# The fifth chunk of keys: 128 rows with zeros in place of 64 rows, in 32 small products of an attention and feed-forward kernel

## The chip, the cores and the metric

The kernel runs on one core of one Trainium2 chip. The metric is the device time of one execution in microseconds (us): the median of several runs of the same program. TensorE is called PE in the profile (PEld for its weight loads), VectorE DVE, ScalarE ACT, GpSimd POOL and SyncE SP.

## What is computed

Eight batches of eight heads, 576 tokens and a head size of 64 go through a linear attention; its output, 4608 tokens of width 512, goes through a feed-forward layer of width 2048 with a gated activation.

```python
q_s = exp(q - max over d);        q_s /= sum over d + 1e-9
k_s = exp(k - max over tokens);   k_s /= sum over tokens + 1e-9
kv  = einsum('bhsd,bhse->bhde', k_s, v)          # sum over 576 tokens
attn = einsum('bhsd,bhde->bhse', q_s, kv)
h = x @ w_in;  g = h * clip(h + 3, 0, 6) / 6;  out = g @ w_out
```

The change touches the line of `kv`: a sum over 576 tokens, which is 4 chunks of 128 tokens and one of 64.

## The kernel before

**The parts.** The 4608 tokens are worked in two ways. The first 1536 go in three blocks of 512 (`j` = 0, 1, 2; `TB` = 512): for each of 16 slices `f` of the hidden width, `gemm1` makes `ph` (12 matmuls of 128x512), an activation and a split into two parts give `gp`, and `gemm2` adds to the output banks `po` (12 matmuls). The other 3072 tokens go in three big blocks of 1024 (`s` = 0, 1, 2) through `phase1` and `phase2`, products with fewer multiplications whose banks are called `x`, `y` and `z`. In block 0 the weights are also brought in and decoded, slice by slice (`load_w`, `decode`): `raw` is what the DMA brings, `m` and `v` are steps of the decoding on ACT and DVE, `w` is the pair of parts that the matmuls use; for odd slices from 3 on the second part of `w` is made on POOL instead of DVE.

**The attention beside it.** The attention of the next block is cut into four units, one for each pair of heads `hp`, and woven into the matmuls of the block that runs. A unit of `attention(j, hp)` loads keys (`kt`), values (`vt`) and queries (`qt`), takes the softmax of the keys (`k_softmax`), turns them on the PE (`pe` for the first four chunks, `pe2` for the fifth), and copies them on ACT into `ke`. Then it turns the queries (`tp`, copied to `qT`), makes `pkv` with `kv_of`, normalises it on DVE (`rk`, then `kv`), makes `px` and splits it into `x`. In `sb_attention`, for the big blocks, the keys come from memory already turned, in chunks of 128 with the last 64 tokens padded by a value whose exponential is zero; `ke` is written whole, by one load, one subtraction and one exponential. `vt` is padded with zeros in memory in both.

**The products in question.** `kv_of` is called 32 times: 4 times for block 0, 4 each for blocks 1 and 2, and 20 times from `sb_attention` (for the first two big blocks two batches in a row for each pair of heads, so 8 double calls; for the last big block one, so 4 single calls). A call has 5 chunks and 2 heads, 10 matmuls; each of these float32 matmuls appears in the trace as two passes, so 20 passes a call and 640 in all. The two heads write to the lower and the upper 64 rows of `pkv`. In chunks 0 to 3 a matmul takes 128 rows, and in chunk 4 only the 64 rows that hold tokens.

**What sets the order.** The order of the instructions on each engine is chosen ahead of time by a scheduler with a model of its own; from block 1 on the matmuls keep the order in which the program writes them (`in_order`), while the other engines, and the PE in block 0, may be reordered. Tiles with `bufs=2` such as `ke` are used in turn: a unit writes its `ke` once the product two units ago has read it. All engines execute their own lists strictly in order.

Of the kernel before, what the change touches and what calls it, by code (L numbers as in the profile page):

```python
# [18 lines left out]
P = 128  # L19
TB = 512  # L20
QD = 32
NC4 = TB // P
# [10 lines left out]
def attention_moe(  # L33
# [15 lines left out]
    nc = tc.nc  # L49

    B, NP, _, S = kT.shape
    D = q.shape[5]
# [7 lines left out]
    NCH = S // P + 1  # L60
    TAIL = S % P
# [14 lines left out]
    def bank_a(name):  # L76
        return ps_a.tile([P, TB], F32, name=name, tag="pa")
# [3 lines left out]
    def ordered(ins):  # L81
        if in_order:
            tc.keep_in_program_order(ins)

    def mm(out, lhsT, rhs, start, stop, goes_on=False):
        ordered(
            nc.tensor.matmul(  # L87
                out, lhsT, rhs, start=start, stop=stop, skip_group_check=goes_on
            )
        )  # L90

    def flip(out, in_):
        ordered(nc.tensor.transpose(out, in_, ident))
# [94 lines left out]
    def kv_of(j, hp, ke, vt):  # L188
        pkv = bank_a("pkv")
        for c in range(NCH):  # L190
            r = slice(0, P if c < NC4 else TAIL)
            for h in range(2):
                hs = slice(h * D, (h + 1) * D)
                mm(pkv[hs, 0 : D + 1], ke[r, c, hs], vt[r, c, h, :], c == 0, c == NCH - 1)
        rk = att.tile([P, 1], F32, name="rk", bufs=2)
        nc.vector.tensor_scalar_add(rk, pkv[:, D : D + 1], EPS)
        nc.vector.reciprocal(rk, rk)
        kv = att.tile([P, P], F32, name="kv", bufs=10)
        nc.vector.scalar_tensor_tensor(
            kv.rearrange("p (h d) -> p h d", h=2),  # L200
            pkv[:, 0:D].rearrange("p (o d) -> p o d", o=1).broadcast_to([P, 2, D]),
            rk,
            mask.rearrange("p (h d) -> p h d", h=2),
            op0=ALU.mult,
            op1=ALU.mult,
        )
        kvs[j, hp] = kv
# [29 lines left out]
    def k_softmax(j, km, ke, kt):  # L237
        nc.vector.tensor_reduce(km, kt, axis=AX.X, op=ALU.max, negate=True)
        nc.scalar.activation(kt, kt, AF.Exp, bias=km)
        yield  # L240
        a = bank_a if j else bank
        pe, pe2 = a("pe"), a("pe2")
        for c in range(NC4):
            flip(pe[:, c * P : (c + 1) * P], kt[:, c * P : (c + 1) * P])
        flip(pe2[0:TAIL, 0:P], kt[:, TB:S])
        nc.scalar.copy(ke[:, 0:NC4].rearrange("p c n -> p (c n)"), pe)
        nc.scalar.copy(ke[0:TAIL, NC4], pe2[0:TAIL, 0:P])

    def attention(j, hp):

        if not j:
            kt, qt, qT, vt, ke = first[hp]
        else:
            kt, ke, vt = load_k(j, hp)
            qt = att.tile([P, TB], F32, name="qt", bufs=1)
            nc.sync.dma_start(qt, q[j, hp])
            qt = qt.rearrange("p (c h d) -> p c h d", c=NC4, h=2)
        km = att.tile([P, 1], F32, name="km", bufs=2)
        ks = k_softmax(j, km, ke, kt)
        next(ks)  # L260
        q_softmax(qt, j > 0, nc.vector if j else nc.gpsimd)
        yield
        next(ks, None)
        tp = (bank_a if j else bank)("tp")
        for c in range(NC4):
            flip(tp[:, c * P : (c + 1) * P], qt[:, c].rearrange("p h d -> p (h d)"))
        if j:
            qT = att.tile([P, TB], F32, name="qT")
        nc.scalar.copy(qT, tp)
        yield  # L270
        kv_of(j, hp, ke, vt)
        yield
        px = (bank_a if j else bank)("px")
        e = SHIFT * j
        for b, lo, hi in ((j - 1, 0, e), (j, e, TB)):
            if lo < hi:
                mm(px[:, lo:hi], kvs[b, hp], qT[:, lo:hi], True, True)
        x_hi, x_lo = x_block(j)
        split(x_hi[:, hp, :], x_lo[:, hp, :], px)
# [51 lines left out]
    def sb_attention(s, hp):  # L331
# [24 lines left out]
        for b, (ke, vt, kb) in new.items():  # L356
            kv_of(b, hp, ke, vt)
# [502 lines left out]
```

## Time and profile before

| | |
|---|---|
| median of 3 runs | 872.07 us (871.47 to 872.77) |
| the profiled execution's own time | 867.29 us |
| its span, first to last instruction | 865.5 us |
| busy: PE, PEld | 819.9, 657.5 us (95%, 76%) |
| busy: DVE, ACT, POOL | 674.1, 459.1, 68.2 us (78%, 53%, 8%) |
| mean granted PE clock | 0.988 |

The profiled execution is 4.8 us shorter than the median of the runs, and its span 1.8 us shorter than its own time. Busy shares are averages over parts with different limits. In a timeline, each row is a start, a length, an engine, a line of the kernel, an operation and its output and inputs; rows of like instructions are merged with their count, so that a merged row's length ends with the end of its last instruction. Matmuls are pipelined: the start of the next one says more about the rate than the length of one. "128\*64" behind a matmul is the number of rows and columns of the PE array that it uses.

### The profile page before, as it was taken

The numbers are of one execution on the slowest core, as the hardware profiler recorded it, in microseconds if no ns is written. First come the engines' busy times: TensorE is split into PE (matmuls) and PEld (weight loads), VectorE is DVE, ScalarE is ACT, GpSimd is POOL, SyncE is SP. The second block draws the span as 40 slices with busy tenths as digits, with TensorE's granted clock in tenths as the row PEclk, the third lists the DMA queues.
The fourth block names the chain that finished last, engine by engine and source line by source line (L and its number), as shares of the span: only waits on it lengthen the run. The fifth ranks groups of instructions, "written<-read, shape, count | busy, mean of one in ns | idle before, by whom it ended". The sixth has DMA issues, their size and how long they took to land.

```text
span 865.5 us, 11820 instructions
## 1 busy us (share of the span) xinstructions
PE 819.9 (95%) x4064; PEld 657.5 (76%) x4064; DVE 674.1 (78%) x1064; ACT 459.1 (53%) x789; POOL 68.2 (8%) x142
## 2 busy tenths in 40 slices
PE   5789998899999998999998999999999999999997
PEld 4568776677887876888786787777788788887886
DVE  7998997885957889579988986588597846648763
ACT  7887665554434445355555553554555634444543
POOL 5111211000100110101102000011000000000000
PEclk9889999999999999999999999999999999999999
DMA  9997654675639661488775566765556775555572
GB/s 368 413 409 265 219 181 161 210 258 201 226 139 316 223 228 58 135 286 266 267 261 176 190 219 226 240 223 172 164 179 195 228 237 194 195 193 191 193 234 87
DMA packets 73531, 190.99 MB, mean 221 GB/s; under 512 B 7168, under 2 KB 19456, under 8 KB 71424
## 3 DMA queue, kind: packets, MB, share of 16 engines
q1 hardware_dynamic: 72896, 189.20, 63.8%
q10 hardware_dynamic: 576, 1.05, 0.3%
q8 instruction: 32, 0.52, 0.3%
q14 instruction: 27, 0.22, 0.1%
HBM read 146.18 MB, written 44.04 MB: 220 GB/s over the span
## 4 chain that ended last, share of the span: by engine, by line
PE 60%; DVE 16%; DMA 5%; issue 4%; ACT 3%; POOL 1%; ACTq 0%; DVEq 0%; SPq 0%; POOLq 0%
PE x L87 25%; PE y L87 10%; PE z L87 9%; PE po L87 7%; PE ph L87 6%; DVE g L498 2%; DVE gp L121 1%; DMA kt<-in_kT_dram 1%; PE px L87 1%; DMA wf<-gp 1%; PE pkv L87 1%; ACT qt L221 1%; DMA out_dram<-v 1%; DMA v<-whole 1%; POOL swap L303 1%
## 5 line engine op out<-in xcount | busy, mean ns | idle before, releaser
L120 ACT CAST gf<-g 128x512 fp32r<-128x512 f32 x168 | 104.2, 624 | 96.4 <-DVE gf L121 48.6
L87 PE MATMUL po<-w,gp 128*128 128x512 f32 x576 | 145.1, 400 | 5.3 <-DVE gp L121 4.3
L87 PE MATMUL ph<-x,w 128*128 128x512 f32 x576 | 144.9, 399 | 2.7 <-POOL w L121 1.3
L121 DVE TENSOR_TENSOR gf<-g,gf 128x512 fp32r<-128x512 f32 x168 | 113.3, 689 | 31.7 <-ACT gf L120 31.0
L87 PEld LDWEIGHTS ph<-x,w 128*128 128x128 f32 x576 | 109.8, 192 | 28.6 <-POOL w L121 1.7
L87 PEld LDWEIGHTS po<-w,gp 128*128 128x128 f32 x576 | 107.3, 190 | 30.2 <-DVE gp L121 5.4
L87 PE MATMUL x<-right,gp 128*128 128x512 f32 x384 | 95.0, 392 | 2.8 <-DVE g L538 2.8
L87 PE MATMUL x<-gf,gp 128*128 128x512 f32 x384 | 89.0, 389 | 0.0
L87 PEld LDWEIGHTS x<-right,gp 128*128 128x128 f32 x384 | 71.6, 188 | 19.1 <-DVE g L538 3.6
L87 PEld LDWEIGHTS x<-gf,gp 128*128 128x128 f32 x384 | 72.1, 188 | 15.0
L497 ACT ACTIVATE g<-ph,three 128x512 f32<-128x512 f32 x48 | 33.0, 691 | 67.7 <-PE ph L87 67.7
L497 ACT ACTIVATE v<-g,three 128x1024 f32<-128x1024 f32 x24 | 27.7, 1154 | 39.6 <-DVE g L542 39.6
L87 PE MATMUL x<-right,left 128*128 128x512 f32 x192 | 47.8, 392 | 0.8 <-DVE g L538 0.8
L87 PE MATMUL y<-right,gp 128*128 128x512 f32 x192 | 48.2, 395 | 0.0
L120 ACT CAST gp<-g 128x512 fp32r<-128x512 f32 x48 | 29.8, 622 | 33.4 <-DVE g L498 30.7
L87 PE MATMUL z<-gf,gp 128*128 128x512 f32 x192 | 45.8, 392 | 0.9 <-DVE gf L121 0.8
L87 PE MATMUL x<-gf,left 128*128 128x512 f32 x192 | 45.9, 392 | 0.8 <-DVE gf L121 0.7
L498 DVE SCALAR_TENSOR_TENSOR g<-g,ph 128x512 f32<-128x512 f32 x48 | 32.4, 677 | 15.4 <-ACT g L497 15.3
L87 PEld LDWEIGHTS z<-gf,gp 128*128 128x128 f32 x192 | 35.7, 188 | 10.0 <-DVE gf L121 2.6
L87 PEld LDWEIGHTS x<-gf,left 128*128 128x128 f32 x192 | 35.7, 188 | 9.7 <-DVE gf L121 2.5
L87 PEld LDWEIGHTS x<-right,left 128*128 128x128 f32 x192 | 35.7, 188 | 8.6 <-DVE g L538 1.3
L87 PEld LDWEIGHTS y<-right,gp 128*128 128x128 f32 x192 | 35.6, 188 | 8.0 <-issue 0.5
(135 smaller groups left out, 1323.3 us busy)
## 6 DMA issues: line engine op xcount, KB each, us to landing
gp<-wf SPq DMA_DIRECT2D x112, 512.0 KB, 3.4
left<-wf SPq DMA_DIRECT2D x56, 512.0 KB, 3.5
raw<-in_w_dram SPq DMA_DIRECT2D x16, 1024.0 KB, 14.2
wf<-gp SPq DMA_DIRECT2D x64, 256.0 KB, 2.6
wf<-w SPq DMA_DIRECT2D x48, 256.0 KB, 4.1
vt<-in_v_dram SPq DMA_DIRECT2D x28, 325.0 KB, 5.5
kt<-in_kT_dram SPq DMA_DIRECT2D x28, 288.0 KB, 3.5
ke<-in_k_dram SPq DMA_DIRECT2D x20, 320.0 KB, 4.9
```

The costliest lines, as they stand in the source:

```text
L87: nc.tensor.matmul(out, lhsT, rhs, start=start, stop=stop, skip_group_check=goes_on)
L120: nc.scalar.copy(hi, src)
L121: engine.tensor_sub(lo, src, hi.bitcast(F32))
L221: nc.scalar.activation(qs[:, i], qs[:, i], AF.Exp, bias=qm[:, i : i + 1], accum_out=qr[:, i : i + 1],)
L303: nc.gpsimd.tensor_copy(swap[r : r + QD], stat[o : o + QD])
L497: nc.scalar.activation(r, h, AF.Relu, bias=three, scale=1.0)
L498: nc.vector.scalar_tensor_tensor(g, r, 6.0, h, op0=ALU.min, op1=ALU.mult)
```

## The change

`kv_of` takes all 128 rows in the fifth chunk as well. In `k_softmax` the upper 64 rows of that chunk of `ke` are set to zero on POOL, since no copy writes them there; the upper rows of `vt` are zero already. In `sb_attention` nothing has to be added.

```diff
     def kv_of(j, hp, ke, vt):
         pkv = bank_a("pkv")
         for c in range(NCH):
-            r = slice(0, P if c < NC4 else TAIL)
             for h in range(2):
                 hs = slice(h * D, (h + 1) * D)
-                mm(pkv[hs, 0 : D + 1], ke[r, c, hs], vt[r, c, h, :], c == 0, c == NCH - 1)
+                mm(pkv[hs, 0 : D + 1], ke[:, c, hs], vt[:, c, h, :], c == 0, c == NCH - 1)
...
         nc.scalar.copy(ke[:, 0:NC4].rearrange("p c n -> p (c n)"), pe)
         nc.scalar.copy(ke[0:TAIL, NC4], pe2[0:TAIL, 0:P])
+        nc.gpsimd.memset(ke[TAIL:P, NC4], 0.0)
```

The number of matmuls stays; 12 memsets are added (blocks 0, 1 and 2, four units each). Because the scheduler lays out the program anew, the lists of the engines also move: on the PE only within block 0, on DVE, ACT and SP mostly there and by a few places in block 1.

POOL's list from block 0's decoding to its end, before (`w_3_422` is the decoded slice 3, and so on; this is the second part of `w` for the odd slices):

```order
L121 TENSOR_TENSOR w_3_422<-v_418,w_3_422 128x2x512
L121 TENSOR_TENSOR w_5_534<-v_530,w_5_534 128x2x512
L121 TENSOR_TENSOR w_7_686<-v_681,w_7_686 128x2x512
L121 TENSOR_TENSOR w_9_821<-v_816,w_9_821 128x2x512
L121 TENSOR_TENSOR w_11_972<-v_967,w_11_972 128x2x512
L121 TENSOR_TENSOR w_13_1074<-v_1069,w_13_1074 128x2x512
L121 TENSOR_TENSOR w_15_1165<-v_1160,w_15_1165 128x2x512
```

The same place after, where the memsets belong to the units of blocks 1 and 2:

```order
L247 MEMSET ke_544 64x128
L121 TENSOR_TENSOR w_3_426<-v_422,w_3_426 128x2x512
L121 TENSOR_TENSOR w_5_539<-v_535,w_5_539 128x2x512
L121 TENSOR_TENSOR w_7_692<-v_687,w_7_692 128x2x512
L247 MEMSET ke_697 64x128
L121 TENSOR_TENSOR w_9_828<-v_823,w_9_828 128x2x512
L121 TENSOR_TENSOR w_11_980<-v_975,w_11_980 128x2x512
L247 MEMSET ke_849 64x128
L121 TENSOR_TENSOR w_13_1082<-v_1077,w_13_1082 128x2x512
L247 MEMSET ke_1289 64x128
L121 TENSOR_TENSOR w_15_1173<-v_1168,w_15_1173 128x2x512
```

Three memsets now stand between the seven splits and one right ahead of them; five others stand further up, at the start of the program, and three behind the last split.

DVE's list near the start of block 0, where the last of the four units there is normalised (`rk_293`, then `kv_296`), before:

```order
L196 TENSOR_SCALAR rk_293<-pkv_282 128x1
L121 TENSOR_TENSOR w_1_334<-v_330,w_1_334 128x2x512
L121 TENSOR_TENSOR x0_311<-px_314,x0_311 128x512
L141 SCALAR_TENSOR_TENSOR v_362<-raw_2_118,m_358 128x1024
L197 RECIPROCAL rk_293<-rk_293 128x1
L121 TENSOR_TENSOR x0_311<-px_318,x0_311 128x512
L145 ISA v_362<-raw_2_118,v_362 128x2048
L199 SCALAR_TENSOR_TENSOR kv_296<-pkv_282,rk_293,mask_80 128x128
```

The same steps on DVE after (`rk_297`, then `kv_300`):

```order
L195 TENSOR_SCALAR rk_297<-pkv_286 128x1
L121 TENSOR_TENSOR x0_315<-px_318,x0_315 128x512
L196 RECIPROCAL rk_297<-rk_297 128x1
L134 TENSOR_SCALAR m_362<-m_362 128x1024
L198 SCALAR_TENSOR_TENSOR kv_300<-pkv_286,rk_297,mask_80 128x128
```

Three big steps of the decoding (`w_1`, and `v` of slice 2 twice) have moved from between `rk` and `kv` to behind them.

The PE's list where block 0 ends and block 1 begins, before (`x_311` is the input of block 0, `x_564` that of block 1, `w_1122` and `w_1165` are slices 14 and 15, `w_306` is slice 0):

```order
L87 MATMUL po<-w_1074,gp 128x512 x4
L87 MATMUL ph<-x_311,w_1165 128x512 x10
L87 MATMUL ph<-x_564,w_306 128x512 x9
L87 MATMUL px<-qT,kv 128x448
L87 MATMUL ph<-x_564,w_306 128x512 x3
L87 MATMUL po<-w_1122,gp 128x512 x12
L87 MATMUL po<-w_1165,gp 128x512 x12
```

And after (`x_315` and `x_569` are the inputs, `w_1130` and `w_1173` slices 14 and 15, `w_310` slice 0):

```order
L87 MATMUL px<-qT,kv 128x448
L87 MATMUL ph<-x_315,w_1173 128x512 x2
L87 MATMUL ph<-x_569,w_310 128x512 x12
L87 MATMUL po<-w_1130,gp 128x512 x9
L87 MATMUL ph<-x_315,w_1173 128x512 x10
L87 MATMUL po<-w_1130,gp 128x512 x3
L87 MATMUL po<-w_1173,gp 128x512 x12
```

The last `px` of block 1's attention has moved ahead of the first `ph` of block 1, and the last ten matmuls of slice 15's `ph` have moved behind that `ph`.

## The prediction

> **What bounds the kernel now.** I read the page first (busy time and the chain that ended last), then a table by stage, then the small products themselves.
>
> ```profile
> PE 819.9 (95%) x4064; PEld 657.5 (76%) x4064; DVE 674.1 (78%) x1064; ACT 459.1 (53%) x789; POOL 68.2 (8%) x142
> PE 60%; DVE 16%; DMA 5%; issue 4%; ACT 3%; POOL 1%; ACTq 0%; DVEq 0%; SPq 0%; POOLq 0%
> ```
>
> The PE is busy for 95% of the span, and 60% of the chain runs over it. A saving on the PE is therefore worth something by default; what matters is in which stage it lies.
>
> ```profile
> 0.00:145.00 145.00, 120.24 (x627) 93.69 (x627) 133.03 (x188) 106.74 (x207) 29.21 (x26) 0.94 0.79 297
> 145.00:365.00 220.00, 209.96 (x1115) 168.69 (x1116) 168.72 (x310) 101.97 (x198) 17.39 (x58) 0.99 0.56 195
> 365.00:530.00 165.00, 161.66 (x832) 129.04 (x831) 144.40 (x228) 88.19 (x134) 16.02 (x40) 1.00 0.71 237
> 530.00:865.00 335.00, 328.05 (x1493) 266.11 (x1492) 227.91 (x339) 162.22 (x250) 5.56 (x18) 1.00 0.60 197
> ```
>
> The columns are the stretch, its length, then busy time and instructions of PE, PEld, DVE, ACT and POOL, the granted clock, the DMA share and GB/s. Up to 145 us (the start and block 0 with its decoding) DVE is the fullest engine, 133.0 of 145 us against 120.2 on the PE. From 145 us on it is the PE, with 700 of 720 us.
>
> The products that the change touches, by shape:
>
> ```profile
> L87 PE MATMUL pkv<-vt,ke 128*64 128x65 f32 x448 | 19.7, 231 | 0.0
> L87 PE MATMUL pkv<-vt,ke 64*64 64x65 f32 x112 | 9.5, 246 | 0.0
> L87 PE MATMUL pkv<-kv 128*64 128x65 f32 x64 | 3.3, 255 | 2.0 <-ACT w L120 2.0
> L87 PE MATMUL pkv<-kv 64*64 64x65 f32 x16 | 1.6, 291 | 0.0
> ```
>
> 448 passes on 128 rows take 19.7 us, 44 ns each; 112 passes on 64 rows take 9.5 us, 85 ns each. The smaller product costs nearly twice as much. Why is seen in the timeline of one double call (40 passes), each row cut so that it begins at the pass in question:
>
> ```profile
> 378.77 0.28 PE L87 MATMUL pkv<-vt,ke 128*64 128x65 f32 x2
> 379.05 0.61 PE L87 MATMUL pkv<-vt,ke 128*64 128x65 f32 x10
> 379.17 0.49 PE L87 MATMUL pkv<-vt,ke 128*64 128x65 f32 x6
> 379.38 0.33 PE L87 MATMUL pkv<-vt,ke 64*64 64x65 f32 x4
> 379.65 0.45 PE L87 MATMUL pkv<-vt,ke 128*64 128x65 f32 x8
> 380.26 0.33 PE L87 MATMUL pkv<-vt,ke 64*64 64x65 f32 x4
> 380.52 0.50 PE L87 MATMUL y<-right,gp 128*128 128x512 f32 x1
> ```
>
> Pass 8 starts at 379.05, pass 12 at 379.17: 0.12 us for four passes, the steady pace. From pass 12 to the first 64-row pass at 379.38 it is 0.21, which is 0.09 too much: the PE stands still before it changes from 128 to 64 rows. From there to the next call at 379.65 it is 0.27 for four passes, 0.15 too much: a slow first pass in the new shape and another standstill on the way back. The first eight passes of the call take 0.28 where 0.23 would be steady, so the slow first pass in a new shape is 0.05.
>
> **The change part by part.**
>
> *The fifth chunk on 128 rows.* Nothing changes its shape inside a call any more. A single call loses the standstill before the fifth chunk and the slow first pass in it, 0.09 + 0.05 = 0.14, call it 0.15 us. On leaving the call, the next big matmul still meets a change of shape, now from 128\*64 to 128\*128 instead of from 64\*64; no row shows it behind such a product, so I bound it: between no cheaper and 0.10 cheaper (the 0.15 of the way back less the slow pass), and take no cheaper, since the row on the way in (378.77) is also such a change and is paid. A double call saves 0.15 twice and in its middle the 0.10 of the way back and the 0.05 of the second call's first pass: 0.45 us. The group rows give less, (85 - 44) ns x 4 = 0.16 us a call and 0.33 for two, since the slow start of the second call is booked there under 128 rows. The number of passes, the weight loads and the later DVE steps stay.
>
> Which of the 32 calls lie on the path? The chain names them:
>
> ```profile
> 161.22 0.88 PE pkv L87 x20
> 177.34 0.88 PE pkv L87 x20
> 213.42 0.88 PE pkv L87 x20
> 318.14 1.76 PE pkv L87 x40
> 378.84 1.76 PE pkv L87 x40
> 553.03 0.88 PE pkv L87 x20
> 569.78 0.88 PE pkv L87 x20
> 586.52 0.88 PE pkv L87 x20
> 603.26 0.88 PE pkv L87 x20
> ```
>
> Seven single calls and two double ones: 7 x 0.15 + 2 x 0.45 = 1.95 us that is on the path for certain. Behind block 0 there are one more single call and six double ones, 0.15 + 6 x 0.45 = 2.85 us, which the chain passes by. Two places of it, and one of these calls:
>
> ```profile
> 264.48 6.49 DMA wf<-gp
> 433.04 5.67 DMA qt<-in_qf_dram
> 264.59 1.83 PE L87 MATMUL pkv<-vt,ke 128*64 128x65 f32 x40
> ```
>
> There the chain runs over DVE and transfers that hand buffers round, while the PE works beside it (210.0 of 220 us, 161.7 of 165 us). An earlier PE hands DVE its inputs earlier as well, and the next stall on the PE is then longer. So between 0 and 2.85 us of it counts; I take half, 1.4, because the table by stage has the PE fullest in both stretches and the chain has DVE there. Sum of the products: 1.95 + 1.4 = 3.35 us, from 1.95 to 4.8. The eight calls before 145 us save another 1.2 us of PE time, which I count at nothing: DVE covers it. If DVE got shorter there, it would count.
>
> *Twelve memsets on POOL.*
>
> ```profile
> L98 POOL MEMSET mask<- x1: 204/204/204, 0.9 to 0.9; 128x128 f32 x1
> L99 POOL MEMSET mask<- x1: 144/144/144, 1.4 to 1.4; 64x64 f32 x1
> 134.20 2.36 POOL L121 TENSOR_TENSOR w<-v,w 128x1024 fp32r<-128x1024 f32 x1 [10.52 <-ACT w L120]
> 134.29 2.82 DVE L121 TENSOR_TENSOR gp<-g,gp 128x512 fp32r<-128x512 f32 x1
> 137.16 1.20 PE L87 MATMUL po<-w,gp 128*128 128x512 f32 x4 [2.04 <-DVE gp L121]
> ```
>
> A memset of 128 elements a row takes 0.20 us. POOL is 8% busy, so its own time is free. It is not free for DVE: while POOL works on a split (134.20 to 136.56), a `gp` split that started with it takes 2.82 us, and the PE waits 2.04 us for it. A memset could hold a DVE instruction in the same way for its own 0.20 us. Only four of the twelve fall into the DVE-bound stretch: 0 to 0.8 us; I take 0.2, since the one long example held DVE in full but most of the 0.2 us windows will fall on instructions that don't compete. As to waiting: a memset waits for the product that read the same buffer two units ago, and behind it on POOL stand the splits of `w`. The orders show each of these products several slices of work ahead of the split behind the memset (`pkv` of two units ago, then at least one `ph` of 12), so I count no wait there, and nobody waits for the memset itself, which is needed only at the end of its unit.
>
> *The new order.* From block 1 on the PE's order is the same. In block 0, two places move. At the start, `kv` of the fourth unit comes sooner on DVE:
>
> ```profile
> 27.26 0.15 DVE L196 TENSOR_SCALAR rk<-pkv 128x1 f32<-128x1 f32 x1
> 31.98 0.35 DVE L199 SCALAR_TENSOR_TENSOR kv<-pkv,rk,mask 128x128 f32<-128x128 f32 x1
> 32.48 2.04 PE L87 MATMUL px<-kq,kv 128*128 128x512 f32 x2 [6.07 <-ACT raw L144]
> ```
>
> The PE waits 6.07 us until 32.48; the wait is put down to ACT, but `kv`, which `px` needs, ends at 32.33. It lies 4.7 us behind `rk`, with three decoding steps in between that now stand behind it. So `px` and the first `ph` could come about 3 us earlier. That is worth nothing by itself, because the decoding steps that gave way set the pace of this block. At its end, the last `px` now has two matmuls of `ph` and nine of the next one between itself and the three that need its result, 11 x 0.227 = 2.5 us of cover, where it had none:
>
> ```profile
> 144.11 0.50 PE L87 MATMUL ph<-x,w 128*128 128x512 f32 x1 [0.68 <-ACT x L120]
> 144.93 0.73 PE L87 MATMUL ph<-x,w 128*128 128x512 f32 x2 [0.33 <-DVE x L121]
> ```
>
> These 0.68 + 0.33 = 1.0 us can go; DVE's list still sets when the rest comes, so I take half, -0.5. The order's whole effect can lie between -3.05 (the 2.04 us above gone as well) and the bound of the slower rival below. On SP a few loads of `raw` and stores of weights change places in block 0; DMA is at 0.79 there and at most 0.71 later, so I count nothing, and up to one transfer's wait if that cover is gone, which falls under the same bounds. The stall that goes leaves `po` of slice 14 as the next that is late, for its `gp` from DVE.
>
> *Sum.* -3.35 + 0.2 - 0.5 = -3.65 us against the profiled execution: 867.29 - 3.65 = 863.6. The median of the runs is 4.8 us above that execution; the same difference against it gives 872.07 - 3.65 = 868.4, which is what I predict.
>
> **A rule weighed.** The rows have a 64-row pass at 85 ns and a 128-row pass at 44. The Trainium skill, page "TensorEngine Tiling (Array Packing)", section "When to Use Tiling", says the reverse of this change: where the contraction is 64 or less, tile the rows in two, for up to twice the speed. By that rule the sum would have the other sign. Its section "Tiling Modes" has the other side too, that changing the mode drains the array; the 0.09 us before the 64-row passes look like that.
>
> **The rivals.**
> 1. *Order gains too*: the products as above, and the waits at the end of block 0 all go: 872.07 - 3.35 - 3.05 + 0.2 = 865.9. For it: both places moved in the right direction. Against: DVE is busy for 133 of 145 us there. Chance 0.14.
> 2. *Mostly hidden*: only the chain's calls count, the memsets cost their 0.8, the order nothing: 872.07 - 1.95 + 0.8 = 870.9. For it: DVE and transfers carry the chain from 254 to 308 and from 391 to 456 us. Chance 0.14.
> 3. *The gap is not the shape's*: the standstill belongs to the last chunk (its late copy into `ke`), and stays; 872.07 + 0.2 to 0.8, say 872.5. Against: the double calls read a `ke` that one exponential wrote whole, and have it too. Chance 0.05.
> 4. *Slower: the new order at the end of block 0.* The last ten `ph` matmuls of slice 15 and all of its `po` now stand behind the first `ph` of block 1, which needs the last split of `x` from DVE. In front of that split DVE waits for the exponentials of the next unit:
>
> ```profile
> DVE qr L233 <- ACT qt L221: 4.1, 2, 2.9
> ```
>
> If that wait (2.9 at its longest) and a POOL-held split (2.04) fall in front of it, and the 10 x 0.227 = 2.3 us of matmuls that used to cover stand behind, block 0 ends up to 7.2 us later: 872.07 - 3.15 + 7.2 = 876.1. It decides the sign from 3.15 us on, and makes the kernel measurably slower from 4.9. Against it: 2.5 us of cover. Chance 0.15.
> 5. *The 64-row passes were the cheaper ones*: if two of them ran side by side, a pass would take 22 ns instead of 44, and filling them up would lose 128 x 22 ns = 2.8 us: 874.9. The 85 ns of the rows speak against it. Chance 0.02. This is what the Trainium skill's rule above would make of the change; no row here agrees with it.
>
> **How the numbers follow.** My forecast has the remaining 0.50. A difference of 0.2%, 1.74 us, is about what a measurement of this kernel can tell from no change. Faster by more than that: forecast and rival 1, 0.64. Within: rivals 2 and 3, 0.19. Slower: rivals 4 and 5, 0.17. The forecast's own range is 866.8 (4.8 saved, memsets free, order -0.5) to 870.3. The range that should hold eight times in ten reaches from 864.5 (rival 1 with 4.8 saved) to 874.5, the middle of rival 4; beyond lie half of rivals 4 and 5 and a small part of rival 1.
>
> **What would show it.** By shape, `pkv` has one form, 640 passes on 128\*64, at 44 to 52 ns, some 29 us instead of 34.1. A single call is about 0.73 us in the chain instead of 0.88, a double one 1.3 instead of 1.76. The first `px` of block 0 comes at about 29 instead of 32.5 us. The last `ph` of block 0's end has no wait for `x`. If the fifth chunk still starts 0.1 us late, rival 3 holds; if the calls shrink and the end does not move, rival 2; if block 1 starts later than 145 us by more than 3, rival 4.

## The result, and the profile after

| | before | after |
|---|---|---|
| median, side by side | 871.47 us (868.63 to 872.77, 11 runs) | 865.66 us (862.18 to 869.36, 11 runs) |
| profiled execution, own time / span | 867.29 / 865.5 us | 868.88 / 867.1 us |

The changed kernel takes 0.9942 of the time before (95% interval 0.9921 to 0.9963): 5.8 us less, where 3.65 were forecast. Repeated later beside other runs of both (e5 below), the ratio was 0.9952 (0.9935 to 0.9970), 4.6 us by medians. The forecast's 0.9958 lies in both intervals.

A warning for whoever subtracts one profile from the other: the profiled execution before was 4.2 us under the median of the runs above, the one after 3.2 over its own, so the two differ by +1.6 us, with the wrong sign. They show how long calls and waits are; the runs have to tell what those are worth.

The products by shape, after (count | busy us, mean ns | idle before):

```profile
L87 PE MATMUL pkv<-vt,ke 128*64 128x65 f32 x560 | 20.7, 225 | 0.0
L87 PE MATMUL pkv<-kv 128*64 128x65 f32 x80 | 3.9, 255 | 2.2 <-ACT w L120 2.2
```

One form is left, 640 passes at 38 ns on average. Now the same double call as shown before, in the timeline, and single and double calls in the chain:

```profile
379.12 1.39 PE L87 MATMUL pkv<-vt,ke 128*64 128x65 f32 x40
380.44 0.73 PE L87 MATMUL y<-right,gp 128*128 128x512 f32 x2
```

```profile
178.41 0.73 PE pkv L87 x20
215.25 0.73 PE pkv L87 x20
379.19 1.32 PE pkv L87 x40
605.05 0.73 PE pkv L87 x20
```

From the call's first pass to the next big matmul it is 380.44 - 379.12 = 1.32 us; before it was 380.52 - 378.77 = 1.75 (the forecast: 0.45 less). A single call has gone from 0.88 to 0.73 us. Worked out for all calls behind block 0, from the start of the first pass of a call to that of its last, it is -0.445 us a double call and -0.149 a single one. The table by stage (same columns as before):

```profile
0.00:145.00 145.00, 119.06 (x635) 91.55 (x636) 131.30 (x186) 105.86 (x205) 32.66 (x36) 0.98 0.80 297
145.00:365.00 220.00, 207.56 (x1107) 166.51 (x1106) 169.89 (x312) 103.00 (x200) 17.32 (x60) 0.98 0.58 195
365.00:530.00 165.00, 160.03 (x825) 127.70 (x824) 142.19 (x225) 86.42 (x133) 15.72 (x40) 0.99 0.73 235
530.00:865.00 335.00, 329.69 (x1503) 267.60 (x1501) 230.03 (x342) 162.96 (x252) 5.55 (x18) 1.00 0.65 197
PE 66%; DVE 11%; DMA 5%; ACT 2%; issue 2%; POOL 0%; SPq 0%; ACTq 0%; DVEq 0%; POOLq 0%
```

The limits are where they were: DVE up to 145 us, then the PE. Up to 145 us the clock is 0.98 in place of 0.94, from 145 to 365 us it is 0.98 in place of 0.99 and from 365 to 530 0.99 in place of 1.00; all three are taken up below.

### The profile page after: what moved, and what is told of

Read it like the earlier page. It is cut to its first block, busy times and chain, and to the rows that moved or that the text cites. A ratio compares the mean times of both kernels' runs of the same rounds, so it can differ in the third digit from the quotient of the medians.

```text
span 867.1 us, 11856 instructions
## 1 busy us (share of the span) xinstructions
PE 816.3 (94%) x4064; PEld 653.4 (75%) x4064; DVE 673.4 (78%) x1064; ACT 458.2 (53%) x789; POOL 71.3 (8%) x154
## 4 chain that ended last, share of the span: by engine, by line
PE 66%; DVE 11%; DMA 5%; ACT 2%; issue 2%; POOL 0%; SPq 0%; ACTq 0%; DVEq 0%; POOLq 0%
PE x L87 26%; PE y L87 11%; PE z L87 10%; PE po L87 9%; PE ph L87 7%; PE px L87 2%; PE pkv L87 2%; DMA out_dram<-v 1%; DVE gp L121 1%; DVE g L498 1%; DMA wf<-gp 1%; DVE gf L121 1%; DMA qt<-in_qf_dram 1%; DVE right L121 1%; DMA v<-whole 1%
## 5 line engine op out<-in xcount | busy, mean ns | idle before, releaser
L87 PE MATMUL po<-w,gp 128*128 128x512 f32 x576 | 147.5, 404 | 7.6 <-DVE gp L121 5.8
```

Source lines behind the costliest of these rows:

```text
L87: nc.tensor.matmul(out, lhsT, rhs, start=start, stop=stop, skip_group_check=goes_on)
```

## The experiments

My theory was that the change of shape inside a call costs PE time, and that this time counts where the PE is fullest. The rivals: that the new order of block 0 made the difference, that the standstill is the last chunk's and not the shape's, and that the memsets matter. A fourth rival is the clock, which changed as well. Calls for batches are the 20 of `sb_attention`, calls for tokens the 12 of blocks 0 to 2; the 8 token calls before 145 us were forecast at nothing. Ratios are against the kernel before, run on the same chip (871.02 us, 35 runs, for e1 to e4; 870.97, 28 runs, for e5 to e8).

### e1: the batch calls alone

```diff
-    def kv_of(j, hp, ke, vt):
+    def kv_of(j, hp, ke, vt, whole_rows=False):
-            r = slice(0, P if c < NC4 else TAIL)
+            r = slice(0, P if c < NC4 or whole_rows else TAIL)
-            kv_of(b, hp, ke, vt)
+            kv_of(b, hp, ke, vt, True)      # in sb_attention
```

No memset; every engine's list is the one before.

> 128 rows in the fifth chunk only in the 20 calls for the big blocks, no memset; all five lists are those of the kernel before, row for row. Theory 'shape' (the change of the PE's shape costs the time): each of 8 double calls is 0.445 us shorter and each of 4 single ones 0.15, as the trace of the changed kernel shows; 2 doubles and the 4 singles were on the chain, 1.5 us for certain, 4.2 at most, with half of the rest 2.8 us faster than before. Theory 'order' (the new order of block 0 brought the 5.8 us): no order changes, so nothing beyond 1 us.

Measured: 866.43 us, 0.9953 (0.9936 to 0.9970), -4.1 us. The shape of these 20 calls alone gives a result as large as e5's whole change, with the order untouched. The clock isn't it: the mean granted clock over the runs is 0.984 in e1, against 0.983 in the runs of before beside it. Their PE time is 8 x 0.445 + 4 x 0.149 = 4.16 us; by the point estimate all of it counts, by the interval (-5.6 to -2.6 us) at least three fifths.

### e2: the token calls, the memsets and the new order

```diff
-    def kv_of(j, hp, ke, vt):
+    def kv_of(j, hp, ke, vt, fill=True):
-            r = slice(0, P if c < NC4 else TAIL)
+            r = slice(0, P if c < NC4 or fill else TAIL)
+        nc.gpsimd.memset(ke[TAIL:P, NC4], 0.0)
-            kv_of(b, hp, ke, vt)
+            kv_of(b, hp, ke, vt, False)      # in sb_attention
```

The lists are those of the changed kernel.

> The memsets and 128 rows only in the 12 calls for blocks 0 to 2; the big blocks' calls stay on 64 rows. All five lists are those of the changed kernel. 'Shape': three or four single calls on the path, 0.45 to 0.6 us, less 0.2 for memsets: 0.3 us faster, not to be told from none. 'Order': most of the 5.8 us, 3 to 6 us faster.

Measured: 870.68 us, 1.0002 (0.9982 to 1.0022). Order, memsets and twelve calls together: nothing, give or take 1.9 us. Rival 1 (the order gains too) and rival 4 (it loses) have no support in it. The mean granted clock of these runs is 0.989 against 0.983, most of it in block 0 (0.98 in place of 0.94 up to 145 us, as in the changed kernel); there DVE is the limit, and the higher clock brought no time.

### e3: the memsets on 64-row products

```diff
+        nc.gpsimd.memset(ke[TAIL:P, NC4], 0.0)
```

All products as before; the scheduler gives block 0 a third order.

> The 12 memsets without the change of the products: no call is shorter, POOL has the twelve more, and the scheduler gives a third order in block 0, neither that of before nor that of the changed kernel. 'Shape': 0 to 0.8 us slower. 'Order': block 0 is a draw of its own, so a difference of up to 3 us of either sign; if this one is faster by 3 us as well, the old order was a poor draw.

Measured: 868.88 us, 0.9971 (0.9957 to 0.9985), -2.5 us. The expectation allowed a draw of up to 3 us of either sign, without a reason for a gain. The memsets only add work, so this is the third order, if it is anything; where it would gain stays open. If it does, a reordering which nobody intended can be worth more than half as much as the change under study.

### e4: the fifth chunk in the middle

```diff
-        for c in range(NCH):
+        chunks = (0, 1, NC4, 2, 3)
+        for c in chunks:
-                mm(pkv[hs, 0 : D + 1], ke[r, c, hs], vt[r, c, h, :], c == 0, c == NCH - 1)
+                mm(pkv[hs, 0 : D + 1], ke[r, c, hs], vt[r, c, h, :], c == chunks[0], c == chunks[-1])
```

64 rows as before, the lists as before; every call now changes its shape twice inside.

> As before, but the 64-row chunk is the third of the five, so every call changes its shape once more; lists as before. 'Shape': the way back inside the call costs 0.15 us more for each of the 16 calls or pairs of calls behind block 0: 9 of these on the chain, 1.35 us, 2.4 at most; 1.9 us slower. 'Order', or a standstill that belongs to the last chunk and not to its shape: no difference, and the standstill stays ahead of the last chunk.

Measured: 871.8 us, 1.0015 (0.9998 to 1.0031), +1.3 us by the ratio. The time settles little; the timeline of the same double call does:

```profile
382.00 1.98 PE L87 MATMUL pkv<-vt,ke 128*64 128x65 f32 x40
383.91 0.50 PE L87 MATMUL y<-right,gp 128*128 128x512 f32 x1
```

And the start of the call, each row cut so that it begins at the pass in question:

```profile
382.00 0.45 PE L87 MATMUL pkv<-vt,ke 128*64 128x65 f32 x8
382.38 0.33 PE L87 MATMUL pkv<-vt,ke 64*64 64x65 f32 x4
382.65 0.28 PE L87 MATMUL pkv<-vt,ke 128*64 128x65 f32 x2
```

From the first pass to the next big matmul it is 1.91 us, against 1.75 before: 0.15 more, in single calls too, for one more change of shape in the body. The 64-row passes now have a chunk of 128 rows behind them and still cost their standstill: the eight passes ahead of them take 0.38 us, where the first eight of a call took 0.28 before, and the four of them take 0.27, as at the old place. So rival 3 (the gap belongs to the last chunk) is out. The exit, from the start of the last pass of a call to that of the next big matmul, is 0.15 us here out of 128\*64 and was 0.15 before out of 64\*64: leaving gets no cheaper, as taken. Behind block 0 the added changes come to 16 x 0.147 = 2.4 us of PE time; the interval (-0.2 to 2.7) holds that, and nothing too.

### e5: the changed kernel again

The changed kernel without an edit, beside e6 to e8.

> The changed kernel itself, beside the others of this call. If the big blocks' calls give 4.1 us (as in the run with these alone) and the 12 token calls, the memsets and the new order together nothing (as in the run with those alone), it is 4.1 us faster than before; if the two don't add, something between 4 and 7.

Measured: 866.35 us, 0.9952 (0.9935 to 0.9970). Against e2, which has the same order, memsets and token calls (each taken by its ratio to before on its own chip), the batch calls are worth 0.50%, 4.4 us: the second reading of the same term.

### e6: e3's order with the batch calls on 128 rows

```diff
-    def kv_of(j, hp, ke, vt):
+    def kv_of(j, hp, ke, vt, whole_rows=False):
-            r = slice(0, P if c < NC4 else TAIL)
+            r = slice(0, P if c < NC4 or whole_rows else TAIL)
+        nc.gpsimd.memset(ke[TAIL:P, NC4], 0.0)
-            kv_of(b, hp, ke, vt)
+            kv_of(b, hp, ke, vt, True)      # in sb_attention
```

> The memsets, with 64 rows in the token calls and 128 rows in the big blocks' calls; all five lists are those of the run with memsets only (the third order). If shape and order simply add: 4.1 + 2.4 = 6.5 us faster than before. If the waits around the transfers hand the gain back: about 4.

Measured: 866.37 us, 0.9951 (0.9932 to 0.9970), -4.6 us. The two gains did not add up to 6.5. Against e3 the batch calls bring 1.7 (by the ratios) to 2.5 us (by the medians), the third and lowest reading, from six runs of e6. The mean granted clock is 0.984 in e6 and in the runs of before beside it, so this gain isn't the clock's either.

### e7: zeros written once

```diff
+        nc.gpsimd.memset(ke[TAIL:P, NC4], 0.0)      # where block 0's four ke are cut
...
-            r = slice(0, P if c < NC4 else TAIL)
...
-                mm(pkv[hs, 0 : D + 1], ke[r, c, hs], vt[r, c, h, :], c == 0, c == NCH - 1)
+                mm(pkv[hs, 0 : D + 1], ke[:, c, hs], vt[:, c, h, :], c == 0, c == NCH - 1)
...
+    kept_ke = []
...
-        ke = att.tile([P, NCH, P], F32, name="ke", bufs=2)
+        while len(kept_ke) < 2:
+            kept_ke.append(att.tile([P, NCH, P], F32, name=f"ke{len(kept_ke)}", bufs=1))
+            nc.gpsimd.memset(kept_ke[-1][TAIL:P, NC4], 0.0)
+        ke = kept_ke[0]
+        kept_ke.reverse()
```

All products on 128 rows as in the changed kernel; the two buffers of `ke` are kept and zeroed at the start, 6 memsets in all, so that none stands among the splits of `w`. Block 0 gets a fourth order.

> The changed kernel with two ke tiles kept for all units, whose upper rows are set to zero once at the start: 6 memsets, all in the first microseconds, none between the splits of w. A fourth order. If the memsets that hold DVE up cost: up to 0.8 us faster than the changed kernel. If only the draw of the order counts: 4.1 us faster than before with a draw of up to 3 us on either side.

Measured: 867.4 us, 0.9968 (0.9951 to 0.9985). No better than the changed kernel. The memsets of the changed kernel in units whose `ke` is a tile of its own (count, minimum/median/maximum in ns, first to last start; block 0's four take 0.20 us each):

```profile
L247 POOL MEMSET ke<- x8: 199/200/633, 2.6 to 179.3; 64x128 f32 x8
```

Most take 0.20 us, two take 0.63 (at 21.5 and 120.7 us, beside a step `m` of the decoding on DVE), and moving them out of the way brings nothing to be measured.

### e8: both heads in one matmul

```diff
-            r = slice(0, P if c < NC4 else TAIL)
-            for h in range(2):
-                hs = slice(h * D, (h + 1) * D)
-                mm(pkv[hs, 0 : D + 1], ke[r, c, hs], vt[r, c, h, :], c == 0, c == NCH - 1)
+            mm(
+                pkv[:, 0 : 2 * (D + 1)],
+                ke[:, c],
+                vt[:, c].rearrange("p h d -> p (h d)"),
+                c == 0,
+                c == NCH - 1,
+            )
...
-            pkv[:, 0:D].rearrange("p (o d) -> p o d", o=1).broadcast_to([P, 2, D]),
+            pkv[:, 0 : 2 * (D + 1)].rearrange("p (h d) -> p h d", h=2)[:, :, 0:D],
```

The idea: half the passes, all on 128\*128, and no change of shape even on entering and leaving a call. The products of one head's keys with the other's values are made and masked off. The memset is added as in the change.

> The changed kernel with one matmul of 128 columns by 130 for both heads in place of two of 64 by 65; the mask takes the cross terms away, as it did the repeated ones. No product changes the shape of the PE any more, so the change on the way in (318 instead of 227 ns to the first pass, and 0.05 us for the slow pass) and on the way out (0.15 us) go too. 'Shape': from the big matmul ahead of a single call to the second one behind it 1.39 us become about 1.15, so 0.24 us for each of 16 calls or pairs, 3.8 us more than the changed kernel, 8 us faster than before, with a draw of the order of 3 us on either side. If a pass of 130 columns costs more than two of 65 side by side: less than 4.

Measured: 872.8 us, 1.0026 (1.0011 to 1.0040): slower, where I expected 8 us less, or under 4 less if a wide pass costs more than two narrow ones. By shape, and the same double call:

```profile
L87 PE MATMUL pkv<-vt,ke 128*128 128x130 f32 x280 | 34.6, 274 | 0.0
382.40 2.40 PE L87 MATMUL pkv<-vt,ke 128*128 128x130 f32 x20
384.56 0.71 PE L87 MATMUL y<-right,gp 128*128 128x512 f32 x2
```

The exit did shrink, from 0.15 to 0.03 us. But one pass of 130 columns takes 110 to 115 ns from start to start, and it replaces two passes of 65 columns that take 58 ns together: 2.16 us for the call instead of 1.32. What I had underrated is that the narrow passes, half of which write to one half of the array's columns and half to the other, start in couples 7 ns apart, one couple every 58 ns; per column that is 0.45 ns against 0.85 for the wide pass, as if two ran side by side. Which passes form a couple the trace doesn't tell. As a check on how PE time counts: against before, and measured from the big matmul ahead of a call to the third one behind it, since the way in is shorter too, the eight double calls and eight single ones behind block 0 cost about 8 x 0.29 + 8 x 0.05 = 2.8 us more on the PE, and 1.8 to 2.3 were measured.

## Why the prediction came out right

**The size of the saving per call: right.** Forecast 0.15 and 0.45 us, measured 0.149 and 0.445; the change of shape is the cause (e1, e4), and rival 3 is out. Rival 5 (64-row passes are the cheaper ones), with the rule of the Trainium skill behind it, is out as well: e1 would have had to be slower. What stands on the same page, "TensorEngine Tiling (Array Packing)", under "Tiling Modes", that switching the mode drains the array, agrees with e4, where one more change costs 0.15 us. One number of "what would show it" was wrong: the forms together were to be busy for 29 us and are for 24.6. The reason I have for it is that lengths of pipelined passes aren't the distances of their starts; all prices above go by starts.

**How much of it counts: probably on the low side, and not settled.** For the batch calls alone the forecast was 4 x 0.15 + 2 x 0.45 on the chain and half of 6 x 0.45 beside it, 2.85 of 4.2 us. The three readings are 4.1 (e1), 4.4 (e5 against e2) and 1.7 to 2.5 us (e6 against e3). Two of them say that nearly all of it counts, though DVE and transfers carry the chain around these calls; each has an interval of 1.5 us or more either way, and the third reading is the half itself, so the half isn't refuted. For the whole change, the mis-sized term is this one if any: with all of it counted, the sum would have been -5.1 us instead of -3.65, nearer to the measured -5.8 and -4.6. A higher clock does not explain the gain: e1 and e6 have it at the clock of before, and e2 has the higher clock without the gain.

The profiled executions allow a reading that leaves block 0 out: from the first single call behind it to the end of the span. Before, after, and the changed kernel again in e5:

```profile
161.15 0.95 PE L87 MATMUL pkv<-vt,ke 128*64 128x65 f32 x20
162.90 0.80 PE L87 MATMUL pkv<-vt,ke 128*64 128x65 f32 x20
160.93 0.80 PE L87 MATMUL pkv<-vt,ke 128*64 128x65 f32 x20
```

The last two are one program, and it reaches this point 2 us apart. Of these, 1.6 us arise at one place: the last twelve `po` of block 0 take 4.71 us from their start to the next `ph` in the one (147.96 to 152.67) and 3.12 in the other (147.61 to 150.73), because a stretch of half the clock fell on them, as described below. What is left to the end of the span:

| batch calls | kernel: from that call to the end, us |
|---|---|
| 64 rows | before 704.4, e2 704.8, e3 704.2 |
| 128 rows | e1 701.2, after 704.2, e5 702.6, e6 701.7, e7 703.3 |

The means are 704.5 and 702.6: 1.9 us, of 4.16 us saved on the PE. With one execution each, and the spread of 3 us within a row, this agrees with either share. How little one execution settles is seen in e4 and e8 as well: with 2.4 and 2.8 us more on the PE they took 709.2 and 711.7 from there, 4.7 and 7.3 above the first mean.

**Where some of it goes back.** Behind the calls the PE meets the same three waits as before. The first and the last of them before, then after:

```profile
275.91 0.30 PE L93 MATMUL pm<-ident,kb 128*128 128x128 f32 x1 [1.89 <-ACT x L368]
456.41 1.66 PE L87 MATMUL x<-right,gp 128*128 128x512 f32 x6 [1.92 <-DVE g L538]
```

```profile
277.55 0.30 PE L93 MATMUL pm<-ident,kb 128*128 128x128 f32 x1 [2.27 <-ACT x L368]
456.37 2.93 PE L87 MATMUL x<-right,gp 128*128 128x512 f32 x6 [2.84 <-DVE g L538]
```

They have grown by 0.38 and 0.92 us (in e1, with the lists of before, by 0.46 and 0.31). For the first wait the other profiles bear it out: it is 1.89 or 1.90 us in the four kernels whose batch calls are on 64 rows (before, e2, e3, e4) and 2.08 to 2.35 in the changed kernel, e1, e5 and e6, so 0.2 to 0.5 us go back there. (In e7 it is 1.74, behind another wait of 1.03.) The PE comes earlier and ACT doesn't: this is the stall that the prediction said would get longer. The last wait can't be read in this way: on 64 rows it is 1.92, but also 1.24 in e2 and 2.70 in e4, against 2.23 to 2.84 on 128 rows.

A second loss was not foreseen. The clock (column before the DMA share) in 10 us around these two places and one between, before and then after:

```profile
274.00:284.00 10.00, 8.11 (x69) 6.54 (x69) 8.63 (x16) 4.00 (x8) 1.69 (x6) 1.00 0.99 355
340.00:350.00 10.00, 7.78 (x27) 5.93 (x26) 7.05 (x9) 2.40 (x4) 0.00 (x0) 0.83 0.14 52
453.00:463.00 10.00, 8.08 (x36) 6.36 (x35) 7.99 (x11) 3.41 (x4) 1.68 (x4) 1.00 0.59 203
```

```profile
274.00:284.00 10.00, 7.73 (x28) 5.95 (x28) 8.53 (x13) 4.33 (x8) 1.37 (x4) 0.83 1.03 377
340.00:350.00 10.00, 7.50 (x32) 5.70 (x32) 8.24 (x9) 3.38 (x5) 0.00 (x0) 1.00 0.12 39
453.00:463.00 10.00, 7.16 (x25) 5.49 (x24) 5.96 (x9) 3.39 (x4) 1.68 (x4) 0.83 0.50 155
```

A clock of 0.83 over 10 us is 3.4 us at half speed, up to 1.7 us lost. Before had one such piece at these places, behind a wait of 2.2 us at 342.8; the profiled execution after had two (and one more at the end of block 0, at 149 us). Which of the three waits is followed by one changes from execution to execution of one program: in e5's it was the second and third. So single executions scatter by whole pieces of up to 1.7 us. That longer waits bring more of them is not shown: there are two at these places in e1, e5 and e6, but also in e3 and e4 with 64 rows, and one in before, e2 and e7. That these pieces are why e3's and e1's gains did not add is a guess; no run took a wait away to test it.

**Block 0: half right.** `kv` came sooner as read from the order, and with it the first `px`, forecast at 29:

```profile
27.98 1.10 PE L87 MATMUL px<-kq,kv 128*128 128x512 f32 x2 [1.88 <-DVE kv L198]
140.69 0.73 PE L87 MATMUL ph<-x,w 128*128 128x512 f32 x2 [0.89 <-DVE x L121]
147.96 2.49 PE L87 MATMUL po<-w,gp 128*128 128x512 f32 x6 [1.53 <-ACT gp L120]
```

As forecast, that was worth nothing: the first call behind block 0 does not start earlier because of it (162.90 and 160.93 against 161.15). At the end of the block the prediction had it wrong. It took half of the 0.68 + 0.33 us of waits for `x` there as gone; instead a `ph` still waits 0.89 us for `x`, and the `po` of slice 15, whose last ten `ph` now stand right ahead of it but for three `po`, waits 1.53 us for its `gp`: 2.42 us in place of 1.01. This is what rival 4 was afraid of, in small; the prediction had named slice 14's `po` as the late one. The start behind the block shows no loss from it. e2 puts order, memsets and token calls together at 0, give or take 1.9 us. The term of -0.5 can't be told from that, and as the wait that it rested on did not go, its part in the forecast is luck if it was gained at all. Rivals 1 and 4, at -3.05 and up to +7.2, do not show. Open is whether e3's third order really gains 2.5 us.

**The memsets: right.** Forecast at 0.2 us, 0 within the error by e2 and e7.

**Rival 2 (mostly hidden)** would have given 870.9 / 872.07 = 0.9987. Both intervals of the changed kernel end below that, at 0.9963 and 0.9970.

## What to carry to other kernels

Keep a run of small products in one shape: a product over half the rows in the midst of others costs two changes of shape, and filling up with zeros that are there anyway costs nothing. Price such an edit by the starts of the matmuls around it in the timeline. Where the PE is the fullest engine of a stretch, count half of a saving there or more even if the chain names another engine: the readings here run from 1.7 to 4.4 of 4.16 us. Where it isn't, none was seen here, within 1.9 us (e2). Don't widen a product to save passes before the timeline shows what the narrow ones take back to back.

## What the runs showed of the hardware

- Into a 64-row product out of 128\*64 the PE stands still for 0.09 us and the first pass in the new shape costs 0.05 more; e4 has one such change more and a call is 0.15 us longer. From the last pass of a call to the next product on 128\*128 it is 0.15 us from start to start, out of 64\*64 (before) as out of 128\*64 (e4).
- Float32 passes of 65 columns, half of them on either half of the array's columns, start every 29 ns on average; one pass of 130 columns over all columns takes 110 to 115 ns (e8).
- Pieces of 3.4 us at half the clock follow waits of 1.4 to 2.8 us, not behind each of them and not in each execution. The changed kernel had one at 149.1 us behind the wait of 1.53, which e5's execution of the same program passed without; e8 had one at 171.3 us behind waits of 1.10 and 1.39 that end 1.7 us apart, at 169.11 and 170.80. A wait of 1.84 us in e8 had one behind it, while in e7 the clock stayed at 1.00 from 453 to 463 us around one of 2.73. These are the last two, e8 first:

```profile
280.41 0.32 PE L93 MATMUL pm<-ident,kb 128*128 128x128 f32 x1 [1.84 <-ACT x L372]
```

```profile
458.26 0.96 PE L87 MATMUL x<-right,gp 128*128 128x512 f32 x3 [2.73 <-DVE g L544]
```

  The Trainium skill, page "TensorE: Matmul & The Clock Gate", section "HAM oscillation — how this bites in real kernels", gives as the rule that the PE should have no gaps above about 3.4 us. Here shorter ones were followed by a drop of the clock.
- A memset of 64x128 on POOL takes 0.20 us. Two of the changed kernel's twelve took 0.63, beside the DVE steps `m` of L134 and L136 (TENSOR_SCALAR on 128x1024, 1.01 and 2.18 us long); two others fell beside the step `v` of L141 (SCALAR_TENSOR_TENSOR, 3.44 and 3.23 us) and took 0.20.
